# Attention into a routed expert layer: a new order inside the value groups, loads that follow a one-value copy, weight sums on VectorE, logits added as a tree

## The chip, the cores and the metric

The kernel runs on one core of one Trainium2 chip. The metric is the device time of one execution in microseconds (us); lower is better. Five engines work on it, each with a queue of its own that is worked off in order: TensorE (PE: matmuls and, as PEld, weight loads), VectorE (DVE), ScalarE (ACT), GpSimd (POOL), and SyncE (SP), which here only issues DMAs. ACT and POOL issue DMAs too.

## The reference

Two stages follow each other. Stage one is causal attention in a sliding window of 128 positions with a linear bias by distance (8 batches, 8 heads, 576 positions, 64 channels a head); stage two is a mixture of 8 experts that sends each of the 4608 tokens to the one expert with the largest logit.

```python
scores = scale * np.matmul(q, k.transpose(0, 1, 3, 2))
mask = (rel >= 0) & (rel < window)                 # rel = query position - key position
scores = np.where(mask, scores + bias[None], -1000000000.0)
attn = np.exp(scores - max); attn = attn / (sum + 1e-09); out = np.matmul(attn, v)
# x: (4608, 512), the heads of a token side by side
logits = x @ w_gate;  expert_idx = np.argmax(logits, axis=1);  gate_w = softmax(logits)[expert_idx]
y = np.maximum(x @ w1[e], 0.0) @ w2[e]             # e = expert_idx of the token
return gate_w[:, None] * y
```

All data are float32.

## The kernel before

**Stages.** The attention runs first, in 16 units. A unit `u` is a pair of batches `bp` (4 of them) and a pair of heads `hp` (4 of them), so four units in a row finish one batch pair. The 9 key blocks of 64 positions of a unit form 4 groups `g`, so there are 64 groups `i = 4u + g`. A loop over `i` (L1173) writes the whole attention out by hand. The expert layer follows: groups of up to 512 tokens of one expert, each multiplied in the manner of Strassen with 7 products where plain blocks need 8 (`strassen1`, `strassen2`), then smaller groups for what did not fit. The products need sums of weight blocks (`w1_sums`, 8 additions of 128x512), which for the first expert are made during the attention.

**A group.** `scores(i)` does the matmuls `sp` (L739), one exponential on ACT (L745) and one multiplication by the decay factors on DVE (L748, or L753 for the last group of a unit); the result is the tile `prob[i]` (`pe`, five buffers). Scores run two groups ahead (`AHEAD = 2`). `values(u, half, kbs)` multiplies `prob` by the values and accumulates in PSUM in `at` (L774). The 576 queries are taken in two halves of 320 and 256 (`QH`); both halves share the one buffer of `at`. `finish(u, half)` copies `at` into `xT` on ACT (L791, L793), sums the probabilities with matmuls against `ind` into a PSUM tile `m` (L806), and adds those to `sumT` (ACT L815 in the first unit of a batch pair, DVE L817 in the others). The tiles `m` have two buffers, which the tasks use as well.

**The order.** `tc.manual_schedule()` keeps every engine's instructions in the order in which the program writes them. In a group the order is: loads, scores of group `i + 2`, perhaps a weight sum, the values of group `i`, then `some()`, which takes the next piece of a list of tasks. In the third group of a unit (`g == 2`) the first half ends and the second begins:

```python
            elif g == 2:
                values(u, 0, (4,))
                finish(u, 0)
                values(u, 1, (3, 4, 5))
```

**Tasks.** After each batch pair `behind(bp)` gives the list of the routing work of that pair, one entry a group: `gate` (L826) and `turn` (L850) bring logits and sums to one row a token; `scale_a`, `scale_b` (L880, whose first instruction is the reduction L882), `scale_c` and `count` work on DVE; `place` uses PE (L925) and DVE; `ones_at` (L950) makes one-hot rows on DVE (L955, nine instructions, and L960); `enlist` (L970) is PE. `row(bp, t)` turns a block of 128 tokens back to rows (PE L984, ACT L986), lets POOL append the scales (L990) and has SP write it to HBM (L992, tensor `x_rows`); its tile `xs` has three buffers. For the third pair (`bp == 2`) the list is squeezed into ten entries. The fourth pair's list is `with_tail`, inside the first expert's products.

**Loads.** Keys, queries and values of a unit are four loads: k and q of 576 KB, and v in two of 288 KB. The tiles have three buffers. Units 0 and 1 are loaded at the start; `load_unit(u + 2)` (L612) follows in the first group of unit `u`, for `u == 0` in its third. All go through SP but the second half of v, which POOL issues. SP waits only for the buffer of the load to be free. Each DMA of SP and ACT also seems to wait for the eighth one before it: the ninth starts at 4.41 us, when a first load has landed. The first expert's `w1` (2 MB, L559) is loaded at unit 5 in one piece, and POOL makes its sums in units 8 to 11. The helper `later` delays the making of a list until its first element is run.

Of the kernel before, what the change touches and what calls it, by code (L numbers as in the profile page):

```python
# [8 lines left out]
F32 = mybir.dt.float32  # L9
I32 = mybir.dt.int32  # L10
AX = mybir.AxisListType.X
# [4 lines left out]
P = 128  # L16
# [441 lines left out]
def kernel(  # L458
# [47 lines left out]
    with ExitStack() as fast:  # L506
# [47 lines left out]
                )  # L554
            return todo

        def load_w1(g, w_pool):
            g["w1"] = w_pool.tile([P, DB, F], F32, name="w1")
            nc.sync.dma_start(g["w1"][:], g["src"][0].rearrange("(a p) f -> p a f", p=P))  # L559

        def load_w2(g, w_pool):
            g["w2"] = w_pool.tile([P, FB, Dm], F32, name="w2")
# [49 lines left out]
        def load_unit(u):  # L612
            load_k(u, 0, S, nc.sync)
            load_q(u, 0, S, nc.sync)
            load_v(u, 0, nc.sync)
            load_v(u, 1, nc.gpsimd)

        load_k(0, 0, 128, nc.sync)
        load_q(0, 0, 256, nc.scalar)
# [5 lines left out]
        load_v(0, 1, nc.scalar, 4, NK)  # L625
        load_k(1, 0, S, nc.sync)
        load_q(1, 0, S, nc.sync)
        load_v(1, 0, nc.sync)

# [247 lines left out]

        def scale_b(bp):  # L880
            lg = small.tile([P, TPB, E], F32, name="lg")
            nc.vector.reduce_sum(lg[:], pr_of[bp].rearrange("p t a h e -> p t e (a h)"), axis=AX)  # L882
            lmax = small.tile([P, TPB], F32, name="lmax")
            nc.vector.reduce_max(lmax[:], lg[:], axis=AX)
            lb = lmax[:].unsqueeze(2).to_broadcast([P, TPB, E])
# [64 lines left out]
        def ones_at(bp):  # L950

            rc = slot_of[bp]
            oc = small.tile([P, TPB, E * NS], F32, name="oc")
            for t in range(TPB):
                nc.vector.tensor_scalar(  # L955
                    oc[:, t, :], K["cols"][:, : E * NS], scalar1=rc[:, 1, t : t + 1],
                    scalar2=K["tok"][:, bp * TPB + t : bp * TPB + t + 1], op0=ALU.is_equal, op1=ALU.mult,
                )
            orow = small.tile([P, TPB, P], F32, name="orow")
            nc.vector.tensor_tensor(  # L960
                orow[:], K["cols"][:, None, :].to_broadcast([P, TPB, P]),
                rc[:, 0, :].unsqueeze(2).to_broadcast([P, TPB, P]), op=ALU.is_equal,
            )
            oh_of[bp] = oc, orow
# [196 lines left out]
        def some():  # L1161
            if tasks:
                for f in tasks.pop(0):
                    f()
# [3 lines left out]
        for i in range(AHEAD):  # L1168
            scores(i)
        route_consts()  # L1170
        load_v(1, 1, nc.gpsimd)
        ws_tasks = later(lambda: w1_sums(fixed[0], nc.gpsimd), 8)
        for i in range(NG):  # L1173
            u, g = divmod(i, 4)
            bp, hp = units[u]
            if g == (0 if u else 2) and u + 2 < len(units):
                load_unit(u + 2)
            if g == 0:
                if u == 5:
                    load_w1(fixed[0], w1_a)  # L1180
                if u == 1:
                    token_numbers()
                if u == 3:
                    table_consts()
            if i + AHEAD < NG:
                scores(i + AHEAD)
            if 8 <= u < 12 and g % 2 == 1:
                ws_tasks.pop(0)()
            if g == 0:
                values(u, 0, (0, 1))  # L1190
                if u < HP - 1:
# [322 lines left out]
```

## Time and profile before

| what | value |
|---|---|
| time, median of 3 runs | 719.11 us (718.06 to 721.3) |
| time of the profiled execution | 721.67 us |
| its span, first to last instruction | 719.9 us |
| mean granted TensorE clock | 0.987 |
| PE busy | 683.4 us, 95% of the span |
| PEld busy | 570.3 us |
| DVE, ACT, POOL busy | 347.1, 225.5, 132.1 us |
| attention on PE | 4.4 to 192.9 us |

The profiled execution stands 2.56 us above the median of the runs, and 1.8 us of it lie outside its span. A start and an end in a line of the profile are counted from the first instruction. In a timeline, the number in square brackets is the idle time of that engine ahead of the instruction, with what ended it; "issue" there means that no wait is visible.

### The profile page before, as it was taken

How to read it: one execution, taken by the hardware profiler on the slowest of the kernel's cores; microseconds unless marked ns; L12 is line 12 of the kernel's file. 1: busy time of each engine (PE TensorE's matmuls, PEld its weight loads, DVE VectorE, ACT ScalarE, POOL GpSimd, SP SyncE). 2: the span in 40 equal slices, each digit the busy share in tenths (PEclk: the TensorE clock that was granted, in tenths of full speed). 3: DMA queues.
4: the chain of work that ended last, by engine and by line, in shares of the span. 5: the costliest groups of instructions: out<-in, count | busy, mean ns of one | idle time of the engine just before them, and what ended most of it. 6: DMA issues, size and time to landing. Idle time of an engine off the chain costs nothing.

```text
span 719.9 us, 14588 instructions
## 1 busy us (share of the span) xinstructions
PE 683.4 (95%) x6204; PEld 570.3 (79%) x6204; DVE 347.1 (48%) x671; ACT 225.5 (31%) x410; POOL 132.1 (18%) x222
## 2 busy tenths in 40 slices
PE   6799999889899999999999999999999999999995
PEld 5677778667678888878887888788788978878892
DVE  3356738775457675443642545255245534433410
ACT  4455546455334223202311321232133023203200
POOL 4320133310200250023022102301220230021020
PEclk9999999999999999999999999999999999999998
DMA  9977876773424961186328236731843482184010
GB/s 249 241 208 264 235 229 182 194 211 109 126 76 166 354 244 45 74 272 226 117 81 305 111 117 199 293 117 27 287 182 117 164 303 77 64 287 153 1 59 8
DMA packets 52091, 122.00 MB, mean 169 GB/s; under 512 B 3679, under 2 KB 14527, under 8 KB 52016
## 3 DMA queue, kind: packets, MB, share of 16 engines
q1 hardware_dynamic: 43120, 95.66, 40.0%
q0 software_dynamic: 7744, 24.43, 10.2%
q8 instruction: 51, 0.84, 0.5%
q10 hardware_dynamic: 1152, 0.88, 0.4%
q14 instruction: 24, 0.20, 0.1%
HBM read 101.79 MB, written 19.96 MB: 169 GB/s over the span
## 4 chain that ended last, share of the span: by engine, by line
issue 57%; PE 22%; POOL 10%; DVE 4%; ACT 3%; DMA 3%; POOLq 0%; SPq 0%; ACTq 0%; DVEq 0%
PE sp L739 6%; PE at L774 6%; POOL out_dram L1353 5%; POOL xg L1090 5%; PE m L984 2%; PE m L806 2%; DMA q_sb<-in_qT_dram 2%; ACT pe L745 1%; PE m L970 1%; PE pair0b L1273 1%; ACT xT L791 1%; PE m L826 1%; DVE pe L748 1%; DMA out_dram<-zo,s_idx 1%; PE m L850 1%
## 5 line engine op out<-in xcount | busy, mean ns | idle before, releaser
L1353 POOL DMA_INDIRECT out_dram<-zo,s_idx x39 | 43.8, 1123 | 384.2 <-DVE zo L1344 283.4
L748 DVE TENSOR_TENSOR pe<-pe,fac 128x768 f32<-128x768 f32 x48 | 48.3, 1007 | 48.7 <-ACT pe L745 48.6
L774 PE MATMUL at<-pe,v_sb 64*64 64x192 f32 (+2 forms) x1408 | 63.0, 292 | 9.1 <-ACT xT L791 6.5
L739 PE MATMUL sp<-q_sb,k_sb 64*64 64x192 f32 (+2 forms) x1152 | 61.7, 330 | 7.5 <-DMA q_sb<-in_qT_dram 6.5
L745 ACT ACTIVATE pe<-sp 128x768 f32<-128x768 f32 x64 | 51.9, 810 | 51.2 <-PE sp L739 45.5
L774 PEld LDWEIGHTS at<-pe,v_sb 64*64 64x64 f32 x1408 | 48.5, 138 | 15.6 <-ACT xT L791 8.6
L739 PEld LDWEIGHTS sp<-q_sb,k_sb 64*64 64x64 f32 x1152 | 42.8, 141 | 19.8 <-issue 6.4
L1090 POOL DMA_INDIRECT xg<-x_rows,g_idx x39 | 42.7, 1094 | 30.6 <-DVE tb L1013 13.2
L806 PE MATMUL m<-pe,ind 128*32 128x192 f32 (+2 forms) x704 | 30.4, 288 | 5.3 <-issue 4.9
L1108 ACT COPY xgT<-m 128x512 f32<-128x512 f32 x39 | 22.8, 585 | 36.8 <-PE m L1107 35.9
L1284 ACT ACTIVATE h<-h 128x512 f32<-128x512 f32 x32 | 20.2, 630 | 40.3 <-DVE h L1283 35.0
L986 ACT COPY xs<-m 128x512 f32<-128x512 f32 x36 | 20.5, 584 | 33.1 <-PE m L984 23.9
L806 PEld LDWEIGHTS m<-pe,ind 128*32 128x32 f32 x704 | 23.4, 110 | 8.3 <-issue 5.8
L501 DVE TENSOR_TENSOR xn<-xg 128x512 f32<-128x512 f32 x39 | 26.1, 685 | 7.6 <-PE m L1107 6.6
L990 POOL COPY xs<-ext 128x16 f32<-128x16 f32 x36 | 10.5, 303 | 85.7 <-DMA x_rows<-xs 40.1
L608 POOL DMA_DIRECT2D v_sb<-in_v_dram x15 | 11.2, 744 | 77.4 <-PE at L774 75.6
L1107 PE MATMUL m<-ident,xn 128*128 128x128 f32 x156 | 23.6, 274 | 0.7 <-DVE xn L501 0.7
L1107 PEld LDWEIGHTS m<-ident,xn 128*128 128x128 f32 x156 | 19.2, 141 | 4.9 <-PE m L1107 0.9
L984 PE MATMUL m<-ident,xT 128*128 128x128 f32 x144 | 22.5, 289 | 0.5 <-DVE hole L1021 0.5
L1385 PE MATMUL pair2a<-w,h 128*128 128x512 f32 x48 | 21.1, 592 | 0.0
L984 PEld LDWEIGHTS m<-ident,xT 128*128 128x128 f32 x144 | 16.9, 150 | 3.9 <-issue 1.7
L791 ACT COPY xT<-at 128x640 f32<-128x640 f32 (+1 forms) x32 | 18.6, 581 | 2.9 <-PE at L774 2.2
(357 smaller groups left out, 1389.8 us busy)
## 6 DMA issues: line engine op xcount, KB each, us to landing
w<-in_moe_w_dram SPq DMA_DIRECT2D x30, 2048.0 KB, 8.9
k_sb<-in_kT_dram SPq DMA_DIRECT2D x15, 576.0 KB, 6.6
q_sb<-in_qT_dram SPq DMA_DIRECT2D x15, 576.0 KB, 7.4
x_rows<-xs SPq DMA_DIRECT2D x32, 264.0 KB, 2.6
v_sb<-in_v_dram SPq DMA_DIRECT2D x15, 288.0 KB, 6.9
v_sb<-in_v_dram POOLq DMA_DIRECT2D x15, 288.0 KB
x_rows<-xs SPq DMA_DIRECT2D x8, 132.0 KB, 2.4
xg<-x_rows,g_idx POOLq DMA_INDIRECT x39
```

Source lines behind the costliest of these rows:

```text
L501: nc.vector.tensor_tensor(to.rearrange("p (h d) -> p h d", h=H), rows[:, :Dm].rearrange("p (h d) -> p h d", h=H), rows[:, Dm : Dm + H].uns ...
L739: nc.tensor.matmul(sp[c * KB : (c + 1) * KB, r, c0 : c0 + n], lhsT=k_sb[u][hs, c, kb * KB : (kb + 1) * KB], rhs=q_sb[u][hs, c, kb * KB : k ...
L745: nc.scalar.activation(pe[:], sp[:, :, :GC], AF.Exp, scale=SCALE)
L748: nc.vector.tensor_tensor(pe.rearrange("p r (k c) -> p r k c", k=2), pe.rearrange("p r (k c) -> p r k c", k=2), fac[:, h0 : h0 + 2, None, ...
L774: nc.tensor.matmul(acc[r * D : (r + 1) * D, c, lo - q0 : hi - q0], lhsT=v_sb[u][c * KB : (c + 1) * KB, kb, r * D : (r + 1) * D], rhs=pe[c ...
L791: nc.scalar.copy(xT[bp][:, hp, : 2 * LQ].rearrange("p (b q) -> p b q", b=2)[:, :, q0 : q0 + n], acc[:, :, :n])
L806: nc.tensor.matmul(sm[32 * j : 32 * j + 32, lo - q0 : hi - q0], lhsT=none[:] if pe is None else ind[:, hp, :], rhs=fac[:, 0, :KB] if pe is ...
L984: nc.tensor.transpose(ps[:, hp * P : (hp + 1) * P], xT[bp][:, hp, t * P : (t + 1) * P], ident[:])
L1090: nc.gpsimd.indirect_dma_start(out=g["xg"][:, j, :], out_offset=None, in_=src, in_offset=bass.IndirectOffsetOnAxis(ap=g_idx[:, g["c0"] + j ...
L1107: nc.tensor.transpose(tp[:, db * P : (db + 1) * P], xn[:, db * P : (db + 1) * P], ident[:])
L1108: nc.scalar.copy(g["xT"][:, :, j * P : (j + 1) * P], tp.rearrange("p (d q) -> p d q", d=DB))
L1353: ins = nc.gpsimd.indirect_dma_start(out=out[:, :], out_offset=bass.IndirectOffsetOnAxis(ap=s_idx[:, g["c0"] + j : g["c0"] + j + 1], axis= ...
```

## The change

The edit has six parts.

1. In the third group of a unit, the last values of the first half and `finish(u, 0)` are moved ahead of the scores of group `i + 2`, and the task of that group is run before the values of the second half.
2. A unit is loaded in four parts, one in each group, all through SP (`load_part`). Ahead of each goes a DMA that copies one value of `prob[i + 1]` into a 1x1 tile `pace`; SP issues it when that tile of probabilities exists. The one tile `pace` is written 65 times. The values of unit 1 are put behind such a copy too. Unit 2 begins at group 0.
3. The first `w1` comes in four pieces of 512 KB, in the second and fourth groups of units 5 and 6.
4. Its eight sums move from POOL to DVE, and from every second group of units 8 to 11 to every group of units 10 and 11.
5. In `scale_b` the reduction over batch-and-head is written as three additions that halve the operand; in `ones_at` nine instructions over 48 columns become two over 9 x 48.
6. `token_numbers` and `table_consts` (POOL) run in group 1 instead of groups 4 and 12.

```diff
+        def load_part(u, g):
+            if g == 0:
+                load_k(u, 0, S, nc.sync)
+            elif g == 1:
+                load_q(u, 0, S, nc.sync)
+            elif g == 2:
+                load_v(u, 0, nc.sync)
+            else:
+                load_v(u, 1, nc.sync)
...
-        load_v(1, 0, nc.sync)
+
+        pace = rte.tile([1, 1], F32, name="pace")
+
+        def no_earlier_than(there):
+            nc.sync.dma_start(pace[:], there)
...
-            nc.vector.reduce_sum(lg[:], pr_of[bp].rearrange("p t a h e -> p t e (a h)"), axis=AX)
+            pr = pr_of[bp]
+            ph = pr[:, :, 0, :, :]
+            nc.vector.tensor_tensor(ph, ph, pr[:, :, 1, :, :], op=ALU.add)
+            nc.vector.tensor_tensor(ph[:, :, 0:2, :], ph[:, :, 0:2, :], ph[:, :, 2:4, :], op=ALU.add)
+            nc.vector.tensor_tensor(lg[:], ph[:, :, 0, :], ph[:, :, 1, :], op=ALU.add)
...
-            for t in range(TPB):
-                nc.vector.tensor_scalar(
-                    oc[:, t, :], K["cols"][:, : E * NS], scalar1=rc[:, 1, t : t + 1],
-                    scalar2=K["tok"][:, bp * TPB + t : bp * TPB + t + 1], op0=ALU.is_equal, op1=ALU.mult,
-                )
+            nc.vector.tensor_tensor(
+                oc[:], K["cols"][:, None, : E * NS].to_broadcast([P, TPB, E * NS]),
+                rc[:, 1, :].unsqueeze(2).to_broadcast([P, TPB, E * NS]), op=ALU.is_equal,
+            )
+            nc.vector.tensor_tensor(
+                oc[:], oc[:],
+                K["tok"][:, bp * TPB : (bp + 1) * TPB].unsqueeze(2).to_broadcast([P, TPB, E * NS]), op=ALU.mult,
+            )
...
-        load_v(1, 1, nc.gpsimd)
-        ws_tasks = later(lambda: w1_sums(fixed[0], nc.gpsimd), 8)
+        no_earlier_than(prob[0][0:1, 0, 0:1])
+        load_v(1, 0, nc.sync)
+        load_v(1, 1, nc.sync)
+        ws_tasks = later(lambda: w1_sums(fixed[0]), 8)
         for i in range(NG):
             u, g = divmod(i, 4)
             bp, hp = units[u]
-            if g == (0 if u else 2) and u + 2 < len(units):
-                load_unit(u + 2)
-            if g == 0:
-                if u == 5:
-                    load_w1(fixed[0], w1_a)
-                if u == 1:
-                    token_numbers()
-                if u == 3:
-                    table_consts()
+            no_earlier_than(prob[min(i + 1, NG - 1)][0:1, 0, 0:1])
+            if u + 2 < len(units):
+                load_part(u + 2, g)
+            if u in (5, 6) and g % 2 == 1:
+                d = 2 * (u - 5) + g // 2
+                load_w1(fixed[0], w1_a, slice(d, d + 1))
+            if i == 1:
+                token_numbers()
+                table_consts()
+            if g == 2:
+                values(u, 0, (4,))
+                finish(u, 0)
             if i + AHEAD < NG:
                 scores(i + AHEAD)
-            if 8 <= u < 12 and g % 2 == 1:
+            if u in (10, 11):
                 ws_tasks.pop(0)()
...
             elif g == 2:
-                values(u, 0, (4,))
-                finish(u, 0)
+                some()
                 values(u, 1, (3, 4, 5))
...
-            some()
+            if g != 2:
+                some()
```

More of the change, by code (lines that the diff above doesn't have):

```diff
@@ L555, in w1_sums, with load_w1 @@
             return todo
-        def load_w1(g, w_pool):
-            g["w1"] = w_pool.tile([P, DB, F], F32, name="w1")
-            nc.sync.dma_start(g["w1"][:], g["src"][0].rearrange("(a p) f -> p a f", p=P))
+        def load_w1(g, w_pool, parts=None):
+            if "w1" not in g:
+                g["w1"] = w_pool.tile([P, DB, F], F32, name="w1")
+            a = parts or slice(0, DB)
+            nc.sync.dma_start(g["w1"][:, a], g["src"][0].rearrange("(a p) f -> p a f", p=P)[:, a])
         def load_w2(g, w_pool):
@@ L610, in load_v @@
             )
[L612 to L616, printed above, removed]
+        def load_part(u, g):
[7 more added lines that the diff above has]
+                load_v(u, 1, nc.sync)
         load_k(0, 0, 128, nc.sync)
```

## The prediction

> **What bounds the kernel now.** I read the slices of the page first, then busy time by stretch, then every wait on PE in the timeline, and for each wait the engine named.
>
> ```profile
> PE   6799999889899999999999999999999999999995
> PEclk9999999999999999999999999999999999999998
> DMA  9977876773424961186328236731843482184010
> ```
>
> Each digit is 18 us. PE is full from the twelfth slice on; what it loses, it loses in the attention. The windows view puts numbers to that (window, length, busy PE, PEld, DVE, ACT, POOL, granted clock, DMA share, GB/s):
>
> ```profile
> 0.00:24.00 24.00, 16.00 (x346) 13.51 (x348) 9.43 (x13) 12.32 (x21) 12.88 (x80) 1.00 0.96 254
> 24.00:32.50 8.50, 4.76 (x90) 3.78 (x84) 2.28 (x4) 1.94 (x3) 0.63 (x1) 0.80 1.00 259
> 32.50:50.50 18.00, 16.93 (x468) 15.18 (x469) 10.26 (x14) 10.28 (x19) 4.44 (x11) 1.00 0.68 205
> ```
>
> A third of the first 24 us and nearly half of the next 8.5 are lost on PE, with the DMA engines full; later it loses 1 us in 17. All its idle time before 240 us comes to 27.5 us. The timeline shows the kinds of it:
>
> ```profile
> 19.51 0.84 PE L806 MATMUL m<-pe,ind 128*32 128x128 f32 x19 [1.00 <-issue]
> ...
> 28.08 0.63 PE L806 MATMUL m<-pe,ind 128*32 128x192 f32 x13 [3.74 <-issue]
> ...
> 46.55 0.89 PE L774 MATMUL at<-pe,v_sb 64*64 64x64 f32 x24 [0.50 <-ACT xT L791]
> ...
> 131.31 0.34 PE L774 MATMUL at<-pe,v_sb 64*64 64x64 f32 x8 [0.82 <-DVE pe L748]
> ...
> 158.17 0.36 PE L925 MATMUL m<-pre,lt_strict 128*128 128x8 f32 x2 [2.27 <-DVE pre L916]
> ```
>
> Two "issue" stops, 4.74 us, stand where the DMA engines have no free time. The trace's packet records have a 16 KB instruction packet of queue q8 at 16.84 to 18.04 and the next at 25.07 to 26.38; PE goes on 1.5 and 1.7 us later. So I read these stops as PE waiting for its own code behind queued loads. After the long one the clock is halved:
>
> ```profile
> 28.90:32.30 3.40, 3.40 (x63) 2.98 (x54) 0.42 (x2) 0.81 (x1) 0.00 (x0) 0.50 0.91 286
> ```
>
> That costs 3.4 x 0.5 = 1.7 us more. The waits view gives the most regular wait (us in total, times, longest):
>
> ```profile
> PE at L774 <- ACT xT L791: 6.5, 13, 0.5
> ```
>
> It is the one buffer of `at`: the second half waits for the copy of the first, and on ACT that copy stands behind the exponential of the scores just made:
>
> ```profile
> 45.10 0.81 ACT L745 ACTIVATE pe<-sp 128x768 f32<-128x768 f32 x1 [0.39 <-PE sp L739]
> 45.81 0.69 ACT L791 COPY xT<-at 128x640 f32<-128x640 f32 x1
> ```
>
> Last, DVE at 128 us, with the weight sums on POOL beside it:
>
> ```profile
> 127.67 1.28 POOL L531 TENSOR_TENSOR w<-w 128x512 f32<-128x512 f32 x1
> ...
> 129.17 1.26 POOL L532 TENSOR_TENSOR ws<-w,ws 128x512 f32<-128x512 f32 x1
> ```
> ```profile
> 128.15 3.11 DVE L748 TENSOR_TENSOR pe<-pe,fac 128x768 f32<-128x768 f32 x1 [0.91 <-ACT pe L745]
> ```
>
> This multiplication takes 0.96 us elsewhere. PE then waits for DVE three times: 0.82, 0.61 and 0.38 us, 1.81 in all.
>
> **The change, part by part.** I sum against the profiled execution, 721.67 us (span 719.9, 1.8 outside), which stands 2.56 above the median of 719.11; the result is carried over by that difference.
>
> *Second half later.* The copy of `at` goes ahead of the exponential and runs beside the sums L806 (about 0.95 us) and the moved scores (0.65); it needs 0.05 + 0.69. The 13 waits, 6.47 us, go. Next is the value group before it: `values(4)` starts 0.65 earlier and needs `prob[i]`. In unit 3 that multiplication ends at 44.40, the values stood at 44.86, and would now stand at 44.21: 0.2 late. Units 1 to 3, which carry no long tasks, are so, 3 x 0.2; where tasks lie between, the margin was 0.85 to 4.9. And 0.5 (the wait at 149.15) lies ahead of the DVE wait at 155.90 and is swallowed there. Gain 6.47 - 0.6 - 0.5 = 5.4.
>
> *That DVE wait grows.* In unit 12 the scores start after 0.22 (values) and 0.9 (sums), so multiplication and `scale_a` behind it on DVE, idle until 149.05, start 0.95 later, and `scale_b`, `scale_c`, `count` up to L916 with them. The tree gives back: reduction 1.22 us, against additions of 288, 144 and 72 elements; 288 is 0.456 (L875), 72 is 0.23, the middle one some 0.31, together 0.95 as they overlap. Loss 0.95 - 0.25 = 0.7.
>
> *Loads behind copies.* Each copy waits for `prob[i + 1]`, ready about a group before, and, as it writes the same `pace`, for the landing of the copy before. The code-fetch stops lose their cause: 4.74 + 1.7 = 6.44 to gain at most. But loads would now be spread over 13 to 40 us, at an estimated 75 to 90% of the DMA engines, and at a share of 0.86 (60 to 80 us) PE still lost 0.55 in 20 us; for 27 us I keep 1.0. New is the chain. No row shows a four-byte copy. The nearest are the writes of `x_rows`, issue to landing:
>
> ```profile
> DMA to landing us min/median/max: 2.0/2.5/8.1
> ```
>
> My estimate from them: a copy on the same rings lands with the load ahead of it, and the next load is by then queued, so two loads overlap; 576 KB drain in 2.3 us at 254 GB/s, v halves in 1.15. Four groups then take 8.0 us if the copy costs 2.0, and 10 if it costs 2.5 with nothing hidden; I take 9, as loads drain meanwhile. PE without stops does units 1 to 3 in 7.4 us (7.8 for unit 3 now), with tasks in 10 to 14. So PE runs short by (9 - 7.4) x 3 = 4.8, less some 3.3 that unit 2's head start covers: 1.5, with bounds of 0 and 5. Behind the copy on SP wait the other loads and the row writes; for a late row write waits the tile `xs`, for it ACT, and for that the exponentials. And the exponential of group i + 6 waits for the copy that read its buffer: three groups of slack, 8 us. In units 5 and 6 the w1 pieces add 2 us twice; I allow 1.0 there. Gain 6.44 - 1.0 - 1.5 - 1.0 = 2.9. The stops at 72.74 and 90.93 (0.72) followed the 2 MB load: 0.4 of it. `load_v` off POOL and the constants in group 1 cost nothing: POOL is idle 8.8 us there, and DVE took 0.96 beside the same instructions at 22.08.
>
> The Trainium skill ("DMA: Bandwidth & Descriptors", Rules for kernel authors) speaks against this part: a transfer under 64 KB is mostly overhead, and the page puts the fixed part of a DMA at 2.0 us. By that the chain runs at 8.0 a unit and the shortage is nil. A second page ("Runtime: NRT & Kernel Launch", Instruction fetch mechanics) says the crossing of a 16 KB code block is mostly hidden. By that rule nothing is to be gained at 18 to 32 us, and the forecast would lose 6.44 - 1.0 of its gain, 714 for the median; the 3.74 us row, ended by such a block, says otherwise, and I go by the row.
>
> *Weight sums.* POOL's eight (1.27 us and more each) go, with the 3.11. DVE gets 8 x 0.685 = 5.5 us in units 10 and 11, where it was busy 16.3 of 20 us (120 to 140), 3.3 of them through POOL (2.15 in the row above, 1.1 in an L932 of 1.34 for 0.23). Net of the one-hot rows: 16.3 - 3.3 + 5.5 x 20/23 - 0.8 = 17: full, not over. Gain 1.4 of the 1.81 (0 if PE meets a late `sumT`).
>
> *One-hot rows.* Nine instructions took 1.93; two of 432 elements take some 0.6 each by the 1.35 of 1152 elements and the 0.685 of 512. At 222 us the chain runs through them to a wait of 1.39 on PE: gain 0.7. In the attention DVE hides it.
>
> *Start.* The 0.85 wait at 12.83 ends when 2.95 MB have come in; POOL's v load is no longer beside: 0.2.
>
> Sum: 5.4 - 0.7 + 2.9 + 0.4 + 1.4 + 0.7 + 0.2 = 10.3. 721.67 - 10.3 = 711.4, and 711.4 - 2.56 = 708.8: I say 709.
>
> **Rivals.** *The chain of copies paces the attention.* Price: if a copy takes 3.6 us a group (the 256 KB load on empty rings took that), a unit takes 14.4 against 11.6 now; over 14 units 39 us, so 758. It decides from 2.9 us a group on. For it: the 8.1 above, and landings of 6.6 to 7.4 for k and q. Against: those were measured behind three loads.
>
> *Nothing moves.* The stops stay, since 90% DMA is enough for them (no 2.9), and the earlier `values(4)` gives half its gain back (2.7): 10.3 - 5.6 = 4.7 from the sum, less 1.5 for the chain and 1.4 for a full DVE: 717.
>
> *More than forecast.* The halved clocks after 158 and 230 us (1.7 each) go as their waits shrink, and the chain costs nothing: 3.4 + 2.5 + 1.0 more, 702.
>
> **Numbers.** Chances: forecast 0.62, more 0.10, nothing moves 0.15, chain 0.13. The forecast's own bounds: stops gone, chain free and every term in full give 5.9 more, 703; the chain at 5, half of the `values(4)` loss again, no gain from POOL or tail give 6 less, 715. The range 700.5 to 719.5 holds these, "more" and "nothing moves", with about 2 us beyond for the spread of the runs (718.06 to 721.3); the chain is left out. A difference of 0.5% (3.6 us) is about what can be told from none. Faster than 715.5: 0.62 + 0.10 = 0.72; within: 0.14 of "nothing moves"; slower: the chain and the rest, 0.14.
>
> **What would show it.** Right: no wait of `at` for `xT` in the second half, no "issue" stop above 1 us before 40 us, clock 1.00 from 28 to 33, L748 never above 1.2 us, PE's `values(4)` waiting 0.2 for DVE in units 1 to 3, a wait above 2.3 at L925. Wrong: PE or ACT waiting for DMAs of `pace`, k or q after 15 us, steps of SP above 2.9 us a group, or long "issue" stops with free DMA engines.

## The result, and the profile after

The changed kernel takes 721.69 us (median of 20 runs, 717.15 to 726.91) beside 719.07 us for the kernel before (20 runs): a ratio of 1.0033, 95% interval 1.0014 to 1.0052. Forecast were 709 and a gain of 1.4%. The profiled execution takes 721.43 us (span 719.7); that of before took 721.67. The same three rows of slices, 18 us a digit:

```profile
PE   6999799979899999999999999999999999999992
PEclk9999899989999999999999999999999999999997
DMA  8777877764415763184358218533823673182010
```

PE is at 9 from the second slice on but for two slices, where before it took twelve, and DMA begins at 8 and 7 where it began at 9. The two are a 7 on PE in the fifth slice (72 to 90 us) and one in the ninth, both with the clock at 8; and the last digit is 2 where before had 5. The same windows as before (window, length, busy PE, PEld, DVE, ACT, POOL, granted clock, DMA share, GB/s), and one where the clock is down:

```profile
24.00:32.50 8.50, 8.43 (x245) 7.63 (x241) 4.57 (x6) 5.59 (x10) 0.00 (x0) 1.00 0.73 212
32.50:50.50 18.00, 17.64 (x435) 13.56 (x431) 10.18 (x14) 9.80 (x17) 0.00 (x0) 1.00 0.74 210
50.50:96.00 45.50, 41.09 (x857) 33.58 (x857) 26.42 (x60) 22.80 (x40) 3.24 (x9) 0.92 0.82 249
...
75.20:82.00 6.80, 6.35 (x84) 5.01 (x88) 2.70 (x4) 3.05 (x6) 1.12 (x3) 0.50 0.82 244
```

From 24 to 32.5 us PE is busy for 8.43 of 8.5 us (4.76 before): the forecast gain is there. Unit 6 (its last matmul of values) ends 9.1 us earlier than before (71.39 against 80.47). Unit 7 ends only 2.3 us earlier. The waits view of PE (us in total, times, longest):

```profile
PE sp L749 <- DMA q_sb<-in_qT_dram: 5.4, 3, 4.3
PE m L816 <- ACT xs L1003: 4.3, 1, 4.3
PE m L939 <- DVE pre L930: 3.7, 1, 3.7
PE m L1124 <- DVE xn L501: 2.1, 3, 1.0
PE m L816 <- issue: 1.7, 1, 1.7
```

The line `at` from `xT`, 6.5 us in 13 waits before, is gone. In its place the second line, one wait of 4.3 us. The timeline follows it back:

```profile
72.87 0.33 SPq L1009 DMA_DIRECT2D x_rows<-xs  x1
75.02 0.59 ACT L1003 COPY xs<-m 128x512 f32<-128x512 f32 x1 [5.81 <-DMA x_rows<-xs]
...
75.65 1.51 PE L816 MATMUL m<-pe,ind 128*32 128x64 f32 x24 [4.26 <-ACT xs L1003]
```

PE wants a tile `m`; ACT has to empty it into `xs` (L1003); that has three buffers, and the first row written is still under way. SP's own queue shows what stands ahead of it (start, us of issue):

```profile
65.16 0.67 SPq L610 DMA_DIRECT2D v_sb<-in_v_dram  x1
65.87 0.63 SPq L561 DMA_DIRECT2D w<-in_moe_w_dram  x1
66.61 0.59 SPq L638 DMA_DIRECT2D pace<-pe  x1
67.30 0.34 SPq L604 DMA_DIRECT2D k_sb<-in_kT_dram  x1
67.73 2.11 SPq L1009 DMA_DIRECT2D x_rows<-xs  x2
```

The first row write is issued at 67.73, right behind 1.4 MB of loads on the same queue, and ACT goes on at 75.02, 7.3 us later, when a row has landed. After the stop the clock is halved for 6.8 us, another 3.4 us lost.

PE's last matmul ends at 706.51 us, 4.43 earlier than before (710.94). The span is shorter by 0.2 us only. SP's waits at the program's last line, after and before, show the rest:

```profile
SPq L1532 <- PEq L1532: 6.6, 2, 6.1
```
```profile
SPq L1510 <- PEq L1510: 3.1, 2, 2.6
```

All engines meet there, and the view names PE's queue; but in the trace's records it is POOL that comes last, with two long instructions of its queue, an INC_SWDGE_SEM and a DRAIN: 1.80 and 6.60 us after, 0.94 and 3.09 before. SP goes on 0.2 us after the DRAIN has ended (719.01 us after, 719.20 before). From PE's last matmul to the last instruction it is 13.2 us after and 8.9 before: 4.24 us more, which no step of the forecast had.

### The profile page after: what moved, and what is told of

Its sections match the earlier page's. It is cut to its first block, busy times and chain, and to the rows that moved or that the text cites. A ratio compares the mean times of both kernels' runs of the same rounds, so it can differ in the third digit from the quotient of the medians.

```text
span 719.7 us, 14743 instructions
## 1 busy us (share of the span) xinstructions
PE 681.8 (95%) x6204; PEld 569.5 (79%) x6204; DVE 343.9 (48%) x659; ACT 225.8 (31%) x410; POOL 112.4 (16%) x199
## 4 chain that ended last, share of the span: by engine, by line
issue 57%; PE 19%; POOL 10%; DVE 6%; DMA 4%; ACT 2%; POOLq 0%; SPq 0%; DVEq 0%; ACTq 0%
POOL out_dram L1375 5%; PE sp L749 5%; POOL xg L1107 5%; PE at L784 4%; PE m L816 3%; PE m L1001 2%; DVE pe L758 2%; DMA q_sb<-in_qT_dram 2%; PE m L987 1%; PE m L836 1%; ACT pe L755 1%; DMA x_rows<-xs 1%; DMA out_dram<-zo,s_idx 1%; PE pair0b L1295 1%; PE pair0a L1295 1%
## 5 line engine op out<-in xcount | busy, mean ns | idle before, releaser
L758 DVE TENSOR_TENSOR pe<-pe,fac 128x768 f32<-128x768 f32 x48 | 45.9, 956 | 54.8 <-ACT pe L755 54.8
L784 PE MATMUL at<-pe,v_sb 64*64 64x192 f32 (+2 forms) x1408 | 61.2, 288 | 2.4 <-issue 1.6
L784 PEld LDWEIGHTS at<-pe,v_sb 64*64 64x64 f32 x1408 | 46.4, 136 | 11.3 <-issue 6.1
L1007 POOL COPY xs<-ext 128x16 f32<-128x16 f32 x36 | 12.4, 356 | 180.0 <-DVE ext L923 79.4
L1003 ACT COPY xs<-m 128x512 f32<-128x512 f32 x36 | 20.6, 584 | 34.4 <-PE m L1001 16.1
L537 DVE TENSOR_TENSOR xs<-xgT 128x512 f32<-128x512 f32 x8 | 5.5, 693 | 27.1 <-ACT xgT L1125 27.1
```

The lines of the kernel that those rows point to most:

```text
L758: nc.vector.tensor_tensor(pe.rearrange("p r (k c) -> p r k c", k=2), pe.rearrange("p r (k c) -> p r k c", k=2), fac[:, h0 : h0 + 2, None, ...
L784: nc.tensor.matmul(acc[r * D : (r + 1) * D, c, lo - q0 : hi - q0], lhsT=v_sb[u][c * KB : (c + 1) * KB, kb, r * D : (r + 1) * D], rhs=pe[c ...
```

## The experiments

The experiments ran in groups, each on one chip with the kernel before beside it. The kernel before took 719.07 us in the result above, and 715.64 (e1 to e4), 715.94 (e5 to e8), 715.79 (e9 to e11, b2), 719.09 (a2, e12 to e14) and 719.93 us (e15, e16) in the groups, so ratios are compared, and small differences only within a group. "PE's end" is PE's last matmul in the profile, "the end" the time from there to the last instruction. PE's end can be compared only between groups with like times of the kernel before: where that takes 719 to 720 us, unit 15 of the attention alone is some 4 us longer (last section).

| run | median us | ratio to before, 95% | PE's end | the end |
|---|---|---|---|---|
| e1 w1 pieces in units 4, 5 | 719.95 | 1.0067 (1.0047 to 1.0087) | 704.29 | 13.2 |
| e2 no copies | 719.53 | 1.0059 (1.0037 to 1.0082) | 703.58 | 13.2 |
| e3b row writes from POOL | 716.93 | 1.0031 (1.0013 to 1.0049) | 697.63 | 16.2 |
| e4 reorder alone | 722.08 | 1.0061 (1.0034 to 1.0088) | 711.75 | 8.8 |
| e5 half of v from POOL | 724.41 | 1.0109 (1.0077 to 1.0140) | 716.75 | 9.0 |
| e6 e3b, v halves from unit 9 from POOL | 713.16 | 0.9962 (0.9939 to 0.9984) | 700.69 | 8.3 |
| e7 w1 pieces in unit 8 | 716.47 | 1.0010 (0.9992 to 1.0028) | 704.09 | 13.2 |
| e8 paced loads alone | 716.17 | 1.0000 (0.9984 to 1.0017) | 700.97 | 13.2 |
| e9 weight sums on DVE alone | 720.83 | 1.0048 (1.0020 to 1.0075) | 710.72 | 8.9 |
| e10 e3b, two v halves from POOL | 708.26 | 0.9902 (0.9865 to 0.9938) | 702.75 | 6.1 |
| e11 e10, placement a group later | 712.54 | 0.9948 (0.9926 to 0.9970) | 704.84 | 6.1 |
| b2 before again | 715.94 | 1.0012 (0.9991 to 1.0033) | 705.35 | 9.0 |
| a2 after again | 720.60 | 1.0018 (0.9997 to 1.0038) | 704.96 | 13.2 |
| e12 e10, weight sums on POOL | 711.12 | 0.9882 (0.9849 to 0.9915) | 701.68 | 6.1 |
| e13 after, weight sums on POOL | 720.83 | 1.0019 (1.0001 to 1.0037) | 704.57 | 13.2 |
| e14 e12 without the reorder | 713.09 | 0.9919 (0.9894 to 0.9945) | 707.48 | 6.2 |
| e15 after, pieces for POOL's count | 723.34 | 1.0043 (1.0014 to 1.0072) | 712.29 | 6.9 |
| e16 e8, pieces for POOL's count | 722.11 | 1.0037 (1.0014 to 1.0060) | 715.44 | 6.9 |

**The wait in unit 7: w1, copies, or the queue?** e1 and e7 move the w1 pieces, e2 takes the copies out, e3b moves the row writes to another queue.

```diff
-            if u in (5, 6) and g % 2 == 1:
-                d = 2 * (u - 5) + g // 2
+            if u in (4, 5) and g % 2 == 1:            # e1
+                d = 2 * (u - 4) + g // 2
```

> The changed kernel with its four w1 pieces loaded in units 4 and 5, ahead of the first row write, and not in 5 and 6. Theory A (the writes of x_rows stand on SP behind copies, loads and w1 pieces; the tile xs comes free late, ACT and with it PE wait 4.26 us at 71.39, and the clock is halved for 6.8 us after it, 7.7 us in all): the wait falls under 1 us, the halved stretch at 75 goes, 714 to 716 us. Rival B (the DMA engines are full from 60 to 80 us, whatever the order on SP): a wait above 3 us stays near 72, 720 to 722. Rival C (the copies themselves cost the gain all along the attention): nothing moves, 720 to 722, with PE late evenly over the units.

Neither A nor C: the wait grew to 7.56 us (71.30 to 78.86). The pieces make the chain of copies late where they stand; the first row write left SP at 71.83, 4.1 us later than in the changed kernel.

```diff
-            if u in (5, 6) and g % 2 == 1:
-                d = 2 * (u - 5) + g // 2
-                load_w1(fixed[0], w1_a, slice(d, d + 1))
+            if u == 8:                                 # e7
+                load_w1(fixed[0], w1_a, slice(g, g + 1))
```

> The changed kernel with its four w1 pieces in the four groups of unit 8, behind the first batch pair's row writes, everything else as it is. Theory A, refined by e1 (the pieces make the chain of copies late, SP comes to the row writes late, and these land late behind loads): copies run at 2.0 to 2.3 us a group up to unit 8, the first row write leaves SP by 67 us, ACT waits for x_rows under 1 us near 71, the clock stays at 1.00 there: 7 us less than the changed kernel, ratio to before 0.993 to 0.995. Rival B (loads and row writes on the same rings are enough for it): the wait stays above 3 us and the ratio at 1.002 to 1.005. The weight sums may come late for the last piece: under 0.5 us.

The row write leaves at 67.68, as the theory had it, and ACT goes on at 74.16, 6.5 us later and not 7.3: a wait of 3.34 us at 71.46, and a second of 2.99 at 119.64, behind loads alone. So w1 was the smaller part, and the half of theory A that blamed a late issue on SP falls: a row that is issued in time, behind a k load, lands late all the same.

```diff
         def no_earlier_than(there):
-            nc.sync.dma_start(pace[:], there)
+            pass                                       # e2
```

> The changed kernel without the one-value copies; loads in the same order on SP, begun as soon as SP comes to them. Theory A: the wait of 4.26 us at 71.39 and its halved clock go (7.7 us), and issue stops of 4 to 5 us with a halved clock come back before 35 us (up to 6.4 us): 718 to 721, about as before. Rival C (the copies cost more than the fetch stops they take away, all along): 712 to 715. A rival for the issue stops (they came from the load on POOL's queue, not from full engines): the stops stay away without the copies, and then 713 to 715 with clock 1.00 from 24 to 32 us.

The picture is theory A's, the ratio worse than it had: the wait in unit 7 is gone, and issue stops of 2.05, 2.96 and 1.38 us before 34 us are back, with another of 1.79 at 85.69. So it is the copies that keep PE's code fetch free; taking v off POOL's queue does not.

```diff
-                nc.sync.dma_start(x_d[r0 : r0 + n, :], xs[p0 : p0 + n, :])
+                (nc.gpsimd if bp < BP - 1 else nc.sync).dma_start(x_d[r0 : r0 + n, :], xs[p0 : p0 + n, :])   # e3b
```

> The changed kernel with the row writes of the attention (batch pairs 0 to 2) issued from POOL, right behind its copy into xs, and not from SP. Theory A (order on SP): writes leave when the row is ready, no wait of ACT L1003 for x_rows above 1 us, halved clock at 75 gone, 714 to 716 us, or up to 718 if POOL's issues (36 of about 1 us) slow DVE beside them. Rival B (the engines are full): the wait of ACT L1003 for x_rows stays above 3 us near 72 and the time at 720 to 722.

```profile
67.25 0.62 POOL L1009 DMA_DIRECT2D x_rows<-xs  x1 [0.34 <-POOL xs L1007]
...
71.70 0.59 ACT L1003 COPY xs<-m 128x512 f32<-128x512 f32 x1 [2.73 <-DMA x_rows<-xs]
72.34 0.86 PE L816 MATMUL m<-pe,ind 128*32 128x64 f32 x24 [1.30 <-ACT xs L1003]
```

The same row, issued at 67.25 from POOL, has landed by 71.66: 4.4 us, not 7.3. The wait is 1.30 us, the clock stays at 1.00 there, and unit 7 ends at 82.35 (88.04 in the changed kernel). So most of the wait comes from the row writes standing on SP, and rival B's forecast (a wait above 3 us whatever the order) fails. The Trainium skill ("DMA: Bandwidth & Descriptors", Queues, rings and completion order) says that each queue has a ring of its own on every DMA engine and that an engine takes turns between the rings; 4.4 against 7.3 us would agree. It is not shown that the queue alone does it, for the load on the engines fell too. The windows from issue to landing, in the changed kernel and in e3b (DMA share and GB/s stand last):

```profile
67.73:75.02 7.29, 3.66 (x86) 2.98 (x78) 3.26 (x12) 0.82 (x2) 0.59 (x2) 1.00 1.02 316
```
```profile
67.25:71.66 4.41, 3.79 (x86) 3.13 (x86) 3.32 (x12) 0.81 (x1) 2.13 (x6) 1.00 0.72 244
```

In e3b SP issues the next k load at 68.87, behind the row; in the changed kernel it did so at 67.30, ahead of it. Nor are POOL's rows quick in themselves: their median to landing in the attention of e3b is 4.7 us, where SP's took 2.9 in the kernel before.

PE's end is 8.9 us earlier than in the changed kernel, but 4.0 of that is the shorter unit 15 of this group: at the end of unit 14 PE is 5.3 us earlier than in the changed kernel's first profile and 4.1 earlier than in its second (a2). The ratio is about the same, for the end takes 16.2 us, 3.0 more.

**The parts alone.** On the kernel before:

```diff
+            if g == 2:                                 # e4
+                values(u, 0, (4,))
+                finish(u, 0)
             if i + AHEAD < NG:
                 scores(i + AHEAD)
...
-                values(u, 0, (4,))
-                finish(u, 0)
+                some()
                 values(u, 1, (3, 4, 5))
...
-            some()
+            if g != 2:
+                some()
```

> The kernel before with one part of the change: values(4), its finish and the copy of at ahead of the scores in the third group, and the tasks behind the scores. Forecast of the sum: 13 waits of 0.5 us go (6.5), values(4) 0.6 late, 0.5 swallowed, the DVE wait at 158 longer by 0.9 to 1.0 (no tree here): 714 to 715 us (ratio 0.994). Rival (the longer DVE wait doubles the halved stretch behind it, as it did in the changed kernel, and takes 1.7 more): 716 to 717.

A miss, on the other side: 0.6% slower. The 13 waits are gone, and the waits view has this instead:

```profile
PE sp L739 <- issue: 6.7, 4, 3.4
...
PE m L806 <- issue: 5.2, 3, 2.2
PE at L774 <- issue: 1.2, 2, 0.7
```

13.2 us of issue stops, against 5.0 in b2 on a chip with the same time for the kernel before. Three lie where there were none:

```profile
113.83 0.31 PE L806 MATMUL m<-pe,ind 128*32 128x64 f32 x4 [2.01 <-issue]
120.39 0.32 PE L739 MATMUL sp<-q_sb,k_sb 64*64 64x192 f32 x1 [1.30 <-issue]
154.15 0.56 PE L739 MATMUL sp<-q_sb,k_sb 64*64 64x192 f32 x8 [1.46 <-issue]
```

The packet records have 16 KB instruction packets of queue q8 that end at 112.45, 118.86 and 152.64; PE goes on 1.4, 1.5 and 1.5 us after each. The loads still come four at a time here (DMA share 0.91 from 110 to 121 us), and a PE that runs on meets the end of its code while the fetch is behind them. That the faster PE is the reason is my reading, and not shown; the stops and the packets are.

```diff
-            if g == (0 if u else 2) and u + 2 < len(units):
-                load_unit(u + 2)
+            no_earlier_than(prob[min(i + 1, NG - 1)][0:1, 0, 0:1])   # e8; no_earlier_than, load_part as in the change
+            if u + 2 < len(units):
+                load_part(u + 2, g)
```

> The kernel before with one part of the change: each load a group behind a one-value copy, all of v on SP, w1 whole in unit 5 as before, the order of scores, values and tasks as before. My sum had 2.9 us of gain for this part. Theory by now: issue stops before 35 us fall from 4.7 to under 2 us and the halved clock at 28.9 goes (4 to 5 us gained on PE by unit 4), a wait of ACT for x_rows of 2 to 8 us appears behind the 2 MB of w1 in units 5 and 6, and under T (row count 10,240) the time after PE's last matmul is 13.1 instead of 8.9 us: ratio to before 1.000 to 1.008. Under the rival of T (tensor operations on POOL decide) the end stays at 8.9 and the ratio is 0.994 to 1.002.

PE's end is at 700.97, 4.4 us before b2's 705.35 (group beside group); the issue stops fall to 1.9 us, no halved clock before 154 us, and the waits for rows are 0.81 and 0.63 us. The end is 13.2 instead of 9.0 us and takes 4.3 back: ratio 1.0000. POOL still makes the weight sums here, so these do not decide the end.

```diff
-        ws_tasks = later(lambda: w1_sums(fixed[0], nc.gpsimd), 8)
+        ws_tasks = later(lambda: w1_sums(fixed[0]), 8)               # e9
...
-            if 8 <= u < 12 and g % 2 == 1:
+            if u in (10, 11):
```

> The kernel before with one part of the change: the eight weight sums on VectorE, one a group in units 10 and 11, none on POOL. Forecast of the sum: 1.4 of the 1.81 us of waits for DVE in units 11 and 12 go, ratio 0.998. Rival: DVE is full from 120 to 140 us and PE waits for it in other places (sumT, gs) for 1.2 us or more, ratio 1.000 to 1.002. Theory T: the loads of v stay on POOL's queue, so 0.94 and 3.09 us at the end although POOL does no tensor operation; the rival of T (POOL's tensor operations make the end short) has 1.80 and 6.60.

The forecast gain of 1.4 is a loss of 0.2 to 0.75%. PE waits for `sumT` 0.88 us at 123.13 and 1.36 at 137.60, 2.24 for the 1.81 that go. The clock is halved for 3.4 us from 124.4 and again from 141.5. The window of 120 to 170 us in e9:

```profile
120.00:170.00 50.00, 43.73 (x790) 34.94 (x779) 34.55 (x90) 22.16 (x39) 13.00 (x18) 0.86 0.58 173
```

Clock 0.86, against 0.97 in the same window of b2. Up to 240 us e9 has 23.8 us of halved clock and b2 6.8; 6.8 of e9's (3.4 in b2) stand at 25.4, ahead of all weight sums, and so are not theirs. The same part undone in the changed kernel:

```diff
-        ws_tasks = later(lambda: w1_sums(fixed[0]), 8)
+        ws_tasks = later(lambda: w1_sums(fixed[0], nc.gpsimd), 8)    # e13, and in e12 on e10
...
-            if u in (10, 11):
+            if 8 <= u < 12 and g % 2 == 1:
```

> The changed kernel with that one part undone: the weight sums on POOL as before. By e9 (ratio 1.005 from the sums alone) it is 2 to 4 us faster than the changed kernel, ratio to before 0.998 to 1.001, waits for sumT and gs at 118 and 138 gone, a multiplication of about 3 us beside two of POOL's sums back; end 13.1 us. Rival (the sums cost nothing here): as the changed kernel, 1.002 to 1.006.

The rival holds: 1.0019, the same as a2 in its group. Whether DVE or POOL makes the sums is worth nothing in the changed kernel.

**The end.** I counted what POOL's queue was given, in contiguous pieces: 128 for an indirect DMA or a row write, 576 for half of v. (The expectations have some 250 too few in every count, for the gate weights; the differences between kernels are the same.)

```diff
             else:
-                load_v(u, 1, nc.sync)
+                load_v(u, 1, nc.gpsimd)                # e5, and load_v(1, 1, ...) too
```

> The changed kernel with the second halves of v for units 1 to 15 loaded by POOL's queue, as in the kernel before. Theory T (the end of the program: POOL's last DRAIN follows from what its queue was given; the row count from there, x 128 rows for an indirect DMA and 576 for a v half, is 10,240 in the changed kernel, 13,700 with the row writes and 18,880 before; INC and DRAIN took 1.80 and 6.60, 2.40 and 9.05, 0.94 and 3.09 us, so it grows to somewhere above 13,700 and then starts anew): with these loads the count is that of before, 0.94 and 3.09 us, and the time after PE's last matmul 8.9 instead of 13.1. Rival (the 8 tensor operations of the weight sums on POOL made it short): 1.80 and 6.60 stay. In the attention: half a v load less on SP's rings at each row write; the wait at 71 falls from 4.3 to 2 or 3 us. Ratio to before 0.995 to 0.998 under T, 1.001 to 1.003 under the rival.

For the end theory T holds: 0.94 and 3.09, 9.0 us. The time is the worst of all, by something that I had as a rival of the forecast and not here: PE waits for q 15.8 us in seven waits (5.4 in three in the changed kernel), SP for the landing of its copies 89.4 us (54.5).

```profile
PE sp L749 <- DMA q_sb<-in_qT_dram: 15.8, 7, 4.3
```
```profile
SPq L638 <- DMA pace<-pe: 89.4, 57, 4.4
```

SP issues a k load at 25.40, 36.01, 46.55 and 58.22: 10.5 to 11.7 us a unit where the changed kernel's chain needs 8.5 to 9.3. Units 1 to 3 need 7.4 on PE. With a load on another queue SP waits longer for each copy (1.57 us on average for 1.11), and the chain of copies does pace the attention.

e6 and e10 have e3b's edit and this one:

```diff
-                load_v(u, 1, nc.sync)
+                load_v(u, 1, nc.gpsimd if u >= 9 else nc.sync)       # e6; u >= 14 in e10
```

> The row writes of the attention from POOL (as in e3b) and the second halves of v for units 9 to 15 from POOL too: row count 13,700 + 7 x 576 = 17,730, past the point where the count seems to start anew. Theory T: the counter at the end is small, INC 0.6 to 0.9 and DRAIN 1.6 to 2.8 us instead of 2.40 and 9.05; the time after PE's last matmul is 7 to 9 us instead of 16.2, PE as in e3b: 8 us less than e3b, ratio to before 0.990 to 0.993. Rival (it grows with the number of POOL's DMAs): INC 2.8, DRAIN 10 to 11, ratio 1.004 to 1.006.

INC and DRAIN take 0.84 and 2.68 us, the end 8.3: theory T holds. By the ratios (0.9962 and 1.0031) it is some 5 us faster than e3b and not 8: a wait for q of 2.83 us stands at 103.34.

> Row writes of the attention from POOL and the second halves of v for units 14 and 15 from POOL: row count 13,700 + 2 x 576 = 14,850, where e3b (13,700) had not started anew and e6 (17,730) had. Theory T: if the restart lies below 14,850, INC is 0.3 to 0.5 and DRAIN 0.5 to 1.2 us, the end after PE's last matmul 5.5 to 7 us instead of 16.2, and with PE as in e3b the ratio to before is 0.985 to 0.989; if it lies above, 2.6 and 9.9 us, ratio 1.002 to 1.004. No wait for q in units 8 to 12 (2.83 us in e6) in either case.

```profile
SPq L1532 <- PEq L1532: 9.1, 2, 8.5
```
```profile
SPq L1532 <- PEq L1532: 1.0, 2, 0.5
```

The first line is e3b's, the second e10's: two loads more on POOL, and 9.05 us have become 0.97 (INC 0.42). The ratio is 0.9902, better than either kernel. PE's end is 5 us later than e3b's: the waits for q (2.84 us at 78.21) and for a row (2.26 at 119.92) differ, and two stretches of halved clock follow them.

```diff
+                for k in range(3):                     # e15, e16: behind the first expert's products
+                    nc.gpsimd.dma_start(
+                        pad_d[k].unsqueeze(2), K["cols"][:].rearrange("p (a b) -> p a b", b=8)[:, :12, 0:1],
+                    )
```

> The changed kernel with three more DMAs on POOL behind the first expert, each of 128 x 12 pieces of 4 bytes into a scratch tensor that nobody reads: row count 10,240 + 3 x 1,536 = 14,850, the count of e10. Theory T: INC 0.42 and DRAIN 0.97 as in e10 and not 1.80 and 6.60, the end after PE's last matmul 6.1 us and not 13.1, the attention as in the changed kernel: 7 us less than it, ratio to before 0.991 to 0.995. Rival (pieces of 4 bytes don't count as rows, or the end hangs on which buffers are used): 1.80 and 6.60, ratio 1.001 to 1.004.

> The paced loads alone (e8) with the same three DMAs on POOL: Theory T: the end 6.2 us and not 13.2, ratio to before 0.989 to 0.993 where e8 had 1.000; so the paced loads are worth what e8 showed in PE's last matmul (4.4 us against the second profile of the kernel before) and 2.8 of the end. Rival: 0.999 to 1.001 as e8.

The end is nearly as T has it: 0.36 and 0.72 us (0.42 and 0.97 in e10), 6.9 us in all. The times are not: the second expert's gather stands behind the three DMAs on POOL's queue, and PE waits 5.19 us in e15 and 3.91 in e16, each with the clock halved behind it. In e16 the attention is slower than in e8 as well, though its program is the same there: waits for rows of 1.34 and 2.08 us (0.81 and 0.63 in e8) and a halved stretch at 82.1; unit 14 ends 2.7 us later.

```profile
285.67 0.69 DVE L502 TENSOR_TENSOR xn<-xg 128x512 f32<-128x512 f32 x1 [5.57 <-DMA xg<-x_rows,g_idx]
...
286.41 0.71 PEld L1125 LDWEIGHTS m<-ident,xn 128*128 128x128 f32 x4 [5.59 <-DVE xn L502]
```

The place was mine, and in e15 it cost what the end gave. A place behind the last gather was not run.

**The DVE wait.** On e10:

```diff
-                return [g3, t3, a, ..., c + n + [lambda: row_out(bp, 0)], p + rs[1:3], o + rs[3:5], e + rs[5:7], [early_table] + rs[7:9],
-                        [lambda: gather(fixed[0], x_d[: 3 * 2 * S, :])]]
+                return [g3, t3, a, ..., c + n + [lambda: row_out(bp, 0)], rs[1:2], p + rs[2:4], o + rs[4:5], e + rs[5:7],
+                        [early_table] + rs[7:9] + [lambda: gather(fixed[0], x_d[: 3 * 2 * S, :])]]   # e11
```

> e10 with the placement of batch pair 2 one group later (a row turned alone between the counting and the placement; the gather joins the last entry, so its group stays). Theory: the wait for DVE at the placement, 3.72 us in unit 12 to 13, falls under 1.5 us and its halved clock of 6.8 us to 3.4 or none: 3 to 6 us less than e10. Rival: DVE's chain only moves on, and the waits for orow, hole and the first xn grow by as much: within 1 us of e10.

The wait of 3.72 at L939 is gone, and PE waits on the same chain at other places, as the rival has it. The ratio is even worse, 0.9948 for 0.9902, though the two intervals overlap:

```profile
151.72 0.34 PE L784 MATMUL at<-pe,v_sb 64*64 64x64 f32 x8 [1.96 <-DVE pe L758]
...
162.80 3.21 PE L987 MATMUL m<-oc,orow 128*128 128x48 f32 x18 [1.64 <-DVE orow L977]
183.53 0.63 PE L1124 MATMUL m<-ident,xn 128*128 128x128 f32 x4 [2.92 <-DVE xn L501]
```

**Both kernels once more, and the best version.** b2 is the kernel before, a2 the changed kernel, both as they were; e12 is e10 with e13's edit, e14 is e12 with e4's edit undone.

> The kernel before once more, for a second profile of it. If the issue stops are the same at every execution: 1.0 and 3.7 us at 18 and 24, 0.5 at 73 and 0.9 at 185, half clock at 28.9. If they hang on how the loads happen to lie: the stops lie elsewhere or have other lengths, and PE's last matmul is 2 to 4 us earlier than the 710.9 of the first profile, which was 2.6 us over its median. The end after it 8.9 us, INC 0.94 and DRAIN 3.09.

The stops before 40 us are the same in kind (1.47 and 2.88 us for 1.00 and 3.74, clock halved at 28.9 again), and units 0 to 14 end within 0.8 us of the first profile. Unit 15 does not: 7.0 us for 12.0. The halved stretches at 185.9 and 230.3 are absent too. PE's end is 5.6 us earlier.

> The changed kernel once more, for a second profile and its ratio beside the other runs. Theory: the wait of ACT for x_rows near 71 (4 us or more, with a halved clock behind it), the DVE wait of 3.7 us near 151 with 6.8 us of halved clock and the end of 13.1 us are there again; the issue stops of unit 15 may be absent, as in the second profile of the kernel before; ratio to before 1.002 to 1.006. Rival (the first profile's waits were chance): one of the three is absent and the ratio is below 1.000.

All three are there: 4.34 us at 71.56 with 6.8 us of halved clock, 3.72 at 149.68 with 6.8 more, the end 13.2 us.

> e10 (row writes from POOL, second halves of v for units 14 and 15 from POOL) with the weight sums back on POOL, one every second group in units 8 to 11, as in the kernel before. Theory (the sums on VectorE cost waits for sumT and halved clocks behind them): 2 to 4 us less than e10, ratio to before 0.984 to 0.988, end after PE's last matmul 6.1 us as in e10. Rival (POOL's sums beside the row writes: rows go out later, ACT waits for x_rows in unit 10 and 11 above 2.3 us): ratio 0.989 to 0.994.

0.9882, faster than both kernels; the sums are not why (e10's interval holds this ratio, in another group). Of the multiplications beside POOL's sums one made PE wait 1.94 us at 120.61.

> e12 without the reorder: values(4), its finish and the copy of at behind the scores again, tasks behind the values. Theory (the reorder is worth its waits where loads are paced and rows do not wait): 13 waits of 0.5 us come back, PE's last matmul 5 to 6 us later than in e12, ratio 0.992 to 0.996. Rival (the reorder is worth nothing, as e4 had it): within 1.5 us of e12.

```profile
PE at L784 <- ACT xT L801: 7.0, 14, 0.5
```

Its waits are back, and PE's end is 5.8 us later than e12's in these two profiles; but 3.8 of that stands at the end of unit 0 already, with a wait for q of 3.44 us at 11.87. The medians of the runs, in one group, differ by 2.0 us, and the intervals overlap. So beside paced loads the reorder may be worth some 2 us, which these runs cannot tell from none; beside loads in bursts it costs 4 to 6.

## Why the prediction was wrong, step by step

Two steps of the forecast failed above all: the 1.0 us allowed for what stands on SP behind the w1 pieces, which measured 7.7, and the move of `load_v` off POOL, which was to cost nothing and lengthened the end by 4.24. The carry-over of -2.56 and the weight sums come next.

- **Second half later, 5.4.** The 13 waits went, as said; that they are time was not shown by the row. e4 loses 4.4 us (ratio) to 6.4 us (medians) with them gone, and e12 gains perhaps 2 on e14, so "gain 6.47 - 0.6 - 0.5" is at least too large. It asked what is late next on ACT and DVE, and not what a PE that runs on asks of the DMA engines; that this is why e4 loses is not shown. The 0.2 us of late `values(4)` in units 1 to 3 hardly occurred (0.07).
- **The DVE wait grows by 0.7.** Right in size: 3.73 us against 2.27 + 0.5 + 0.7; 3.72 in e12 and 2.12 in e14, without the reorder. (In e4 it stays at 2.31, with an issue stop of 1.46 us just ahead of it.) The clock behind it was left out: halved for 6.8 us in both profiles of the changed kernel, 3.4 before, so 1.7 more. In e1, e6 and e13 it is 3.4 behind the same wait. The tree brought 0.15 by the same wait in e14 and b2 (2.12 and 2.27), against 0.25.
- **Loads behind copies, 2.9 (with 0.4 and 0.2 more).** Right in sign and near in size: 4.4 in e8. Of its issue stops one of 1.75 us stayed, at 16.30 (0.74 in a2). The chain was not short in the changed kernel (1.5 allowed); its rival showed up only in e5. Mis-sized is "in units 5 and 6 the w1 pieces add 2 us twice; I allow 1.0 there": 4.26 us of wait and 3.4 of halved clock, 7.7. I had named the line (row write, `xs`, ACT, exponentials) and priced it by the pieces' issue on SP; its price is the landing of a row behind loads in SP's queue, 7.3 us; in e7, without w1, it was still 6.5, and in e3b, from POOL, 4.4.
- **Weight sums, 1.4.** Nothing in the changed kernel (e13), a loss alone (e9): "full, not over" counted DVE's work over 20 us and not the order in it. Waits of 0.88 and 1.36 us took the place of 1.81.
- **One-hot rows, 0.7.** Right: the wait at L987 (L970 before) fell from 1.39 to 0.62 us.
- **The end, not in the sum.** `load_v` off POOL "cost nothing", I wrote, since POOL is idle there. What POOL's queue is given is paid for when the program ends, in a time that can fall as well as grow with it: here 4.24 us more.
- **Carried over by -2.56.** This needed the changed kernel's profile to stand as far over its median as that of before. It stood at it (721.43 and 721.69): its two halved stretches stand in both profiles of it, where two of the four of the kernel before (185.9 and 230.3) are absent from b2.

Against the forecast's 10.3, PE's end moved by 4.43. The wait for rows (6.7 over its allowance), the halved clock behind the placement (1.7) and the weight sums (1.4) make 9.8; 1.5 of unneeded chain shortage and two halved stretches absent from this profile (3.4) come off: 4.9 of the 5.9 missing. This is an account and not a proof: it counts the reorder in full, and with the 2 us of e12 and e14 it would explain more than is missing. Then the end takes 4.24 of the 4.43, and the carry-over that did not hold is the other 2.6.

The rival "nothing moves" came nearest (717), by luck: most of the stops did go. The one rival that was slower, the chain of copies, was not what made it slower.

## What to carry to other kernels

A wait of 0.5 us that comes 13 times is not yet 6.5 us: ask what an engine that no longer waits will need sooner, its code included. Try small writes that give a buffer free on another queue than the big loads; here that brought PE 4 to 5 us further by the end of unit 14. And look past the last matmul: what is moved on or off POOL's DMA queue can come back at the program's end.

## What the runs showed of the hardware that I had not expected

**POOL's end goes like a saw.** The two last long instructions of POOL by what its queue was given (pieces, the gate weights' 512 included, and DMAs); the runs of a row agree to 0.01 us:

| pieces | DMAs | runs | INC_SWDGE_SEM, DRAIN, us |
|---|---|---|---|
| 10,496 | 80 | after, a2, e1, e2, e7, e8, e13 | 1.80, 6.60 |
| 13,952 | 110 | e3b | 2.40, 9.05 |
| 15,104 | 112 | e10, e11, e12, e14 | 0.42, 0.97 |
| 15,104 | 83 | e15, e16 | 0.36, 0.72 |
| 17,984 | 117 | e6 | 0.84, 2.68 |
| 19,136 | 95 | before, b2, e4, e5, e9 | 0.94, 3.09 |

It grows by 2.45 us of DRAIN for the 3,456 pieces of e3b, and starts anew between 13,952 and 15,104. What is reset there the traces do not show. That POOL's tensor operations do not decide is shown by e8 and e9, and e15 shows that other DMAs than loads and rows count as well. The count of pieces is not the whole measure: 15,104 gives two values, and from 17,984 to 19,136 DRAIN grows by 0.41 us only. If each DMA counts 16 more and 16,384 is taken off where it is passed, the rows stand at 48 (e15), 512 (e10), 3,472 (e6), 4,272 (before), 11,776 (after) and 15,712 (e3b), and both times rise in this order. That is a fit to six points, and no run tests it.

**A stop of 1 to 4 us costs up to 3.4 more.** In the attention the clock is halved in stretches of 3.4 or 6.8 us. The Trainium skill ("TensorE: Matmul & The Clock Gate", What's actually happening) has the clock fall after an idle window of about 3.4 us. The stretches agree with that window; the trigger does not: 0.88 us of wait at 123.13 in e9 were followed by a halved clock at 124.4, and 2.01 us at 111.82 in e4 were not. An estimate of the cost of a wait should have this as its upper end.

**Unit 15 has two lengths.** It takes 7.0 to 7.9 us in eleven of the twelve profiles of the three groups where the kernel before takes 715.6 to 715.9 us (e11, with 2.92 us of wait for `xn` in it, takes 11.0), and 10.1 to 12.8 in all eight where it takes 719 to 720, whatever the kernel. The windows of unit 15 in a2 and in b2, with the same work of PE:

```profile
175.78:187.32 11.54, 9.21 (x185) 6.51 (x188) 4.90 (x7) 3.77 (x7) 3.73 (x4) 1.00 0.35 95
```
```profile
179.81:186.81 7.00, 6.93 (x185) 5.74 (x188) 4.81 (x7) 3.66 (x7) 3.65 (x4) 1.00 0.60 154
```

In a2, at full clock and a DMA share of 0.35, PE issues in small groups; four gaps of 0.2 to 0.9 us that the trace puts down to issue make 1.5 us of the 4.5. The difference is of the size of the 3.3 us between the groups' times of the kernel before. What PE waits for there stays open.
